# An attention, expert-mix and gated-product chain on one core: who straightens whole tiles, where positions are clipped, and the order of gathers and stores at the end of the expert stage

## The chip, the cores and the metric

The kernel runs on one core of one Trainium2 chip. A NeuronCore has five engines with queues of their own: PE (TensorE, matrix products into PSUM), DVE (VectorE), ACT (ScalarE), POOL (GpSimd) and SP (SyncE, which here only issues transfers). Each engine works through its own list in order; an instruction that has to wait holds up all that stands behind it on its engine. The metric is the device time of one execution in microseconds (us), lower being better.

## The reference, cut to what matters

Everything is float32. Linear attention (8 batches, 8 heads, 576 rows, 64 columns) makes x with 4608 rows and 512 columns. A router sends every row to two of eight experts, and a gated product follows:

```python
noisy_logits = x @ w_gate + log1p(exp(x @ w_noise)) * noise
top2, top2_w = two largest of noisy_logits, softmax over the two
for e in range(8):                      # w1[e]: 512x1024, w2[e]: 1024x512
    out[mask] += top2_w[mask, k, None] * (np.maximum(x[mask] @ w1[e], 0.0) @ w2[e])
a = x @ w1; b = x @ w2                  # the second stage: moe2_w1, moe2_w2
return ((a * b) @ w3) @ w_out
```

## The kernel before

**Stages.** The generator `front` does attention and routing. The experts run as *units*: a unit is two or three tiles of 128 routed rows of one expert (`cuts`, L662). Expert 0 is split into two halves: its first half list (rows of the first 18 row tiles) is units 0 and 1 and starts while attention still runs; its last half list is units `nu-2` (three tiles) and `nu-1` (two tiles), the last two of all. Experts 1 to 7 lie between, four units each. The gated product (`gated`) then runs over 12 blocks of three row tiles. Every product is three float32r matmuls (`mm3`, L97 to L100: high times high, high times low, low times high), so each operand is first split in two by `split` (ACT writes the high part, DVE the low part).

**Where rows come from.** Attention writes its rows to the DRAM tensor `X`; experts fetch rows by an indirect DMA on POOL's queue. Units 0 to 2 fetch a whole row tile in one indirect DMA (L709, `na` = 2, so `u <= na`); later units fetch four quarters of 128 columns (`gather_quarters`, L137), laid out so that one DVE transpose per tile suffices (L117). A whole tile is instead *straightened* first: POOL copies it with its columns regrouped into a tile `xr` (L122), PE transposes it in four pieces into PSUM (L124), and `split` makes `xT` of it. `xr` takes its buffers from the pool of the expert outputs (`y`, two buffers).

**The expert stage.** `unit` does `product1` eight times (steps 0 to 7, PSUM tiles `ph`, of which four can be in flight from unit 2 on), then `product2` per tile (steps 8, 9, 10, PSUM tiles `py`), whose result ACT copies to a tile `y` (L749) and stores to the DRAM tensor `Y` from ACT's own queue (L751). Between steps, `turn` straightens or transposes tiles of the next unit, `wstep` splits the next weights, and `hook_conv` does pieces of a conversion of the second stage's weights on DVE (L628 to L645).

**What leads over to the gated product.** `columns` (L877) runs once, behind unit `na+3`: it clips the rows' places in `Y` (`pos`, L879), spreads them over the partitions with 32 small matmuls (`replicate`, L132) and makes the gather indices `posq`. `gather2(i)` (L945) fetches the two expert results of each row of row tile i out of `Y`: eight indirect DMAs on POOL. `take(i)` weighs and adds them (ACT L957, DVE L960), transposes and splits them, and then issues `gather2(i + 2)`. The program calls `gather2(0)` and `gather2(1)` inside `w34` (a product of the second stage's weights, before unit `nu-2`), `take(0)` at step 9 of unit `nu-2`, `take(1)` at step 2 and `take(2)` at step 7 of unit `nu-1`, and the takes of block b+1 behind steps 1, 5 and 8 of block b (`CFB`).

**What orders the work.** The framework puts a wait between two accesses of the same tile or DRAM tensor, in the order in which the program writes them. A gather reads `Y` as a whole, so it waits for the stores written ahead of it, and a store waits for the gathers written ahead of it. Up to the end of unit 1 a scheduler merges the engines' lists; from L872 on the order is the program's own.

Of the kernel before, what the change touches and what calls it, by code (L numbers as in the profile page):

```python
# [8 lines left out]
F32 = mybir.dt.float32  # L9
# [6 lines left out]
ALU = mybir.AluOpType  # L16
# [8 lines left out]
D = NH * DH  # L25
E = 8
F = 1024
CU = 10
ROWS = 128 * CU
# [7 lines left out]
RTAIL = 4  # L37
PUMP = 3
CFB = {1: 0, 5: 1, 8: 2}
GROUPS = [(0, 9), (9, 15), (15, 18), (18, 26), (26, 32), (32, 35), (35, 36)]  # L40


@with_exitstack
def moe_chain_kernel(ctx, tc, q, kt, v0, v1, noise, wg, w1, w2, mw1, mw2, mw3t, mwo, out):
    nc = tc.nc
    V, A, P, G = nc.vector, nc.scalar, nc.tensor, nc.gpsimd
# [14 lines left out]
    pos = const.tile([128, NT, 2], F32, name="pos")  # L61
# [15 lines left out]
    rawp = pool(main, "rawp", 2)  # L77
# [32 lines left out]
    def by_chunk(rows):  # L110

        return rows.rearrange("p (i c d) -> p c i d", i=4, c=4)

    def transp(src, xt, t, quarters):
        if quarters:
            pt = extra["xq"].tile([128, 4, 4, 32], F32, name="xq", tag="xq")
            V.transpose(out=pt, in_=src.rearrange("p (j c d) -> p c j d", j=4, c=4))  # L117
            pt = pt.rearrange("p c j t -> p c (j t)")
        else:
            pt = ptr.tile([128, 4, 128], F32, name="pt", tag="pt")  # L120
            rows = late["y"].tile([128, 4, 4, 32], F32, name="xr", tag="y")
            G.tensor_copy(out=rows, in_=by_chunk(src))  # L122
            for c in range(4):
                P.transpose(pt[:, c, :], rows[:, c].rearrange("p i d -> p (i d)"), ident)  # L124
        split(pt, xt[:, 0, :, 128 * t:128 * t + 128], xt[:, 1, :, 128 * t:128 * t + 128])
# [16 lines left out]
    def front(st):  # L142
# [287 lines left out]
        def route(gi):  # L430
            i0, i1 = GROUPS[gi]
            n = i1 - i0
# [124 lines left out]
        for i in range(NT + 1):  # L557
# [7 lines left out]
            if i:  # L565
                q_logit(i - 1)
                if gi < len(GROUPS) and i == GROUPS[gi][1]:
                    rq.append(route(gi))
# [89 lines left out]
    def wtile(p):  # L658
        return p.tile([128, 2, 1024], F32R, name="w", tag="w")
# [11 lines left out]
    na = 2 * NS  # L671
    extra = {}
    raws, xg, xts = {}, {}, {}
# [44 lines left out]
    def xpose(u, t):  # L718
        if t == 0:
            xts[u] = late["xt"].tile([128, 2, 4, 384], F32R, name="xT", tag="xT")  # L720
        transp(xg.pop((u, t)), xts[u], t, u > na)

    def turn(u, step):
        n, e, part, j0, nt, N, first, last = units[u]
# [28 lines left out]
    events = {}  # L753
# [122 lines left out]

    def columns():  # L877

        V.tensor_scalar(out=pos, in0=pos, scalar1=float(E * ROWS - 1), scalar2=None, op0=ALU.min)  # L879
        V.tensor_scalar(out=posq, in0=replicate(pos.rearrange("p n k -> p (n k)")), scalar1=4.0,  # L880
                        scalar2=quart[:, 0:1], op0=ALU.mult, op1=ALU.add)
        V.tensor_copy(out=gwq, in_=replicate(gw.rearrange("p n k -> p (n k)")))
# [16 lines left out]
    def wscratch(key, k, p):  # L899
        w = wtile(p)  # L900
        nc.sync.dma_start(out=w.rearrange("p s f -> p (s f)").bitcast(F32), in_=WS[k])
        wt[key] = w
# [39 lines left out]
    BT = 3  # L942
    x2s = {}

    def gather2(i):  # L945
        if i >= NT:
            return
        for k in range(2):
            y = extra["g2"].tile([128, D], F32, name="yg", tag="yg")
            gather_quarters(y, Y, posq[:, :, 2 * i + k:2 * i + k + 1])  # L950
            x2s[i, k] = y

    def take(i):
        y0, y1 = x2s.pop((i, 0)), x2s.pop((i, 1))
        for j in range(4):
            c = slice(128 * j, 128 * j + 128)
            A.mul(out=y0[:, c], in_=y0[:, c], mul=gwq[:, j, 2 * i:2 * i + 1])  # L957
        for j in range(4):
            c = slice(128 * j, 128 * j + 128)
            V.scalar_tensor_tensor(out=y0[:, c], in0=y1[:, c], scalar=gwq[:, j, 2 * i + 1:2 * i + 2],  # L960
                                   in1=y0[:, c], op0=ALU.mult, op1=ALU.add)
        b, t = divmod(i, BT)
        if t == 0:
            xts["g", b] = late["xt"].tile([128, 2, 4, 384], F32R, name="xT", tag="xT")
        transp(y0, xts["g", b], t, True)
        gather2(i + 2)

    def load_b():
        for j in range(4):
# [1 line left out]

    nu = len(units)
    events[nu - 3, 7] = [w34_begin]
    events[nu - 2, 9] = [lambda: take(0)]
    events[nu - 1, 2] = [lambda: take(1)]
    events[nu - 1, 7] = [lambda: take(2), load_b]
    for u in range(na, nu):
        if units[u][2] == 2 and units[u][7]:
            unit_open(u, hook_conv)
        else:  # L980
            unit(u, hook_conv, True)
        if u == na:
            turns["py"].append(ptr)
        if u == na + 3:
            columns()
        if u == nu - 3:
            w34()
    for j in range(4):
        wscratch(("w", j), 20 + j, late["w2"])

    most = nc.values_load(nmax[0:1, 0:1], min_val=0, max_val=T)

    def gated():
        N = 128 * BT
        nblk = NT // BT
        ap_ = extra["a"]
        for b in range(nblk):
            xt = xts.pop(("g", b))
            pT = late["ht"].tile([128, 2, 8, 384], F32R, name="hT", tag="hT")
            for fb in range(8):  # L1000
                f0 = 128 * (fb % 2)
                for g in ("a", "b"):
                    ps = bank_of("ph", [128, 384])
                    w = wt[g, fb // 2].rearrange("p s (c f) -> p s c f", c=4)
                    for c in range(4):
                        mm3(ps, w[:, 0, c, f0:f0 + 128], w[:, 1, c, f0:f0 + 128], xt[:, 0, c, :], xt[:, 1, c, :],
                            c == 0, c == 3)
                    if g == "a":
                        a = ap_.tile([128, 384], F32, name="a", tag="a")
                        A.copy(out=a, in_=ps)  # L1010
                    else:
                        V.tensor_tensor(out=a, in0=a, in1=ps, op=ALU.mult)  # L1012
                        split(a, pT[:, 0, fb, :], pT[:, 1, fb, :])
                if b + 1 < nblk and fb in CFB:
                    take(BT * (b + 1) + CFB[fb])
            for m in range(BT):
                po = bank_of("py", [128, 512])
                for fb in range(8):
                    w = wt["w", fb // 2].rearrange("p s (c d) -> p s c d", c=2)
                    mm3(po, pT[:, 0, fb, 128 * m:128 * m + 128], pT[:, 1, fb, 128 * m:128 * m + 128],  # L1020
                        w[:, 0, fb % 2, :], w[:, 1, fb % 2, :], fb == 0, fb == 7)
                y = late["y"].tile([128, D], F32, name="y", tag="y")
                A.copy(out=y, in_=po)
                r = N * b + 128 * m
                nc.sync.dma_start(out=out[r:r + 128, :], in_=y)
                if b + 1 < nblk and m + 8 in CFB:
                    take(BT * (b + 1) + CFB[m + 8])

    gated()
    main.close()  # L1030

# [124 lines left out]
```

## Time and profile before

| | us |
|---|---|
| median of three runs (1743.00 to 1746.36) | 1745.32 |
| the profiled execution | 1746.65 |
| its span, first to last instruction | 1744.7 |
| PE busy | 1665.7 (95%) |
| DVE, ACT, POOL busy | 886.3, 572.5, 690.7 |

The sum of the prediction is made against the profiled execution, whose span leaves 1.95 us around it. PE's granted clock is 0.982 of full speed over the whole span. All times of rows below are counted from the span's start. Unit 0 begins near 153 us, unit 2 near 262, unit 6 near 375, unit `nu-2` near 1066, unit `nu-1` near 1099 and the gated product near 1131. A timeline row ends in brackets with the idle time of the engine just before it and what ended it.

### The profile page before, as it was taken

The page shows a single profiled execution, that of the slowest core. Times are in us where ns is not written, and L with a number is a line of the kernel's source. Part 1 is how long each engine was busy: PE and PEld are TensorE (multiplying, and loading weights), DVE is VectorE, ACT ScalarE, POOL GpSimd, SP SyncE. Part 2 cuts the span into 40 slices and gives each one's busy share as a digit, 9 for nine tenths or more (in the row PEclk, how much of TensorE's full clock was granted, in tenths as well). Part 3 has the DMA queues.
Part 4 walks back from the last instruction along what each step waited for, and adds up shares of the span by engine and source line. Part 5 has one row for each costly group of instructions (what it writes and reads, how often), then busy time and mean ns, then how long its engine had stood idle before and what let it go on. Part 6 is the DMA issues. An engine that isn't in the chain of part 4 may idle for free. (4 is left out here: it accounts for less than half of the span.)

```text
span 1744.7 us, 26430 instructions
## 1 busy us (share of the span) xinstructions
PE 1665.7 (95%) x9903; PEld 1519.5 (87%) x9903; DVE 886.3 (51%) x2251; ACT 572.5 (33%) x1195; POOL 690.7 (40%) x706
## 2 busy tenths in 40 slices
PE   6887979989999999999999999899999999999998
PEld 5666868988989989899998988789999999999997
DVE  6699735766567575774767513233323233332321
ACT  6553322333233333332333312232223233232321
POOL 4456334414334143341443420544454454444500
PEclk9898989999999999999999999999999999999999
DMA  8875344535355253553545484521111111111100
GB/s 297 263 238 173 110 151 150 175 104 168 112 169 172 86 177 124 162 157 104 166 152 173 154 318 165 187 101 43 49 53 48 52 54 35 44 48 52 50 23 20
DMA packets 130060, 221.51 MB, mean 127 GB/s; under 512 B 18560, under 2 KB 65792, under 8 KB 126848
## 3 DMA queue, kind: packets, MB, share of 16 engines
q1 hardware_dynamic: 95040, 152.07, 26.7%
q0 software_dynamic: 19072, 39.88, 8.4%
q10 hardware_dynamic: 15808, 27.71, 4.3%
q8 instruction: 85, 1.39, 0.3%
q14 instruction: 55, 0.45, 0.1%
HBM read 152.22 MB, written 67.37 MB: 126 GB/s over the span
## 5 line engine op out<-in xcount | busy, mean ns | idle before, releaser
L98 PE MATMUL ph<-xT,w 128*128 128x384 f32 (+1 forms) x1792 | 576.2, 322 | 13.6 <-DVE hT L739 9.4
L99 PE MATMUL ph<-xT,w 128*128 128x384 f32 (+1 forms) x1792 | 574.6, 321 | 0.8 <-DVE xT L95 0.7
L100 PE MATMUL ph<-xT,w 128*128 128x384 f32 (+1 forms) x1792 | 574.0, 320 | 0.0
L137 POOL DMA_INDIRECT xg<-X,idxq x288 | 282.5, 981 | 467.7 <-DVE xq L117 395.3
L137 POOL DMA_INDIRECT yg<-Y,posq x288 | 295.0, 1024 | 364.9 <-DVE yg L960 209.0
L98 PEld LDWEIGHTS ph<-xT,w 128*128 128x128 f32 x1792 | 339.8, 190 | 18.6 <-DVE hT L739 11.8
L100 PE MATMUL py<-w,hT 128*128 128x512 f32 x904 | 353.0, 390 | 0.4
L99 PE MATMUL py<-w,hT 128*128 128x512 f32 x904 | 352.3, 390 | 0.0
L98 PE MATMUL py<-w,hT 128*128 128x512 f32 x904 | 352.2, 390 | 0.0
L99 PEld LDWEIGHTS ph<-xT,w 128*128 128x128 f32 x1792 | 339.4, 189 | 3.3 <-DVE xT L95 1.5
L100 PEld LDWEIGHTS ph<-xT,w 128*128 128x128 f32 x1792 | 339.5, 189 | 0.0
L100 PEld LDWEIGHTS py<-w,hT 128*128 128x128 f32 x904 | 169.7, 188 | 37.4 <-DVE hT L739 2.0
L99 PEld LDWEIGHTS py<-w,hT 128*128 128x128 f32 x904 | 169.7, 188 | 34.0
L98 PEld LDWEIGHTS py<-w,hT 128*128 128x128 f32 x904 | 169.7, 188 | 33.9
L1012 DVE TENSOR_TENSOR a<-a,ph 128x384 f32<-128x384 f32 x96 | 53.0, 552 | 281.6 <-PE ph L100 263.5
L739 DVE SCALAR_TENSOR_TENSOR hT<-ph,hT 128x256 fp32r<-128x256 f32 (+1 forms) x256 | 120.5, 474 | 103.4 <-ACT hT L738 100.4
L738 ACT ACTIVATE hT<-ph 128x256 fp32r<-128x256 f32 (+1 forms) x256 | 107.2, 426 | 158.1 <-PE ph L100 143.6
L95 DVE TENSOR_TENSOR xT<-xq,xT 128x512 fp32r<-128x512 f32 x108 | 74.8, 693 | 154.9 <-ACT xT L94 154.9
L749 ACT COPY y<-py 128x512 f32<-128x512 f32 x77 | 45.2, 587 | 258.0 <-PE py L100 214.4
L94 ACT CAST xT<-xq 128x512 fp32r<-128x512 f32 x108 | 67.0, 620 | 138.7 <-DVE xq L117 129.2
L94 ACT CAST hT<-a 128x384 fp32r<-128x384 f32 x96 | 49.4, 514 | 182.3 <-DVE a L1012 182.3
L95 DVE TENSOR_TENSOR w<-raw,w 128x1024 fp32r<-128x1024 f32 x72 | 88.8, 1236 | 11.7 <-ACT w L94 11.6
(203 smaller groups left out, 1529.5 us busy)
## 6 DMA issues: line engine op xcount, KB each, us to landing
raw<-in_w_dram SPq DMA_DIRECT2D x72, 512.0 KB, 4.1
w<-WS SPq DMA_DIRECT2D x24, 1024.0 KB, 6.6
WS<-hl SPq DMA_DIRECT2D x80, 256.0 KB, 2.8
Y<-y ACTq DMA_DIRECT2D x77, 256.0 KB, 2.5
k<-in_kt_dram SPq DMA_DIRECT2D x32, 288.0 KB, 4.4
q<-in_q_dram SPq DMA_DIRECT2D x36, 256.0 KB, 4.0
X<-xt SPq DMA_DIRECT2D x36, 256.0 KB, 2.4
out_dram<-y SPq DMA_DIRECT2D x36, 256.0 KB, 2.1
```

Source lines behind the costliest of these rows:

```text
L94: A.copy(out=hi, in_=src)
L95: V.tensor_tensor(out=lo, in0=src, in1=hi.bitcast(F32), op=ALU.subtract)
L98: P.matmul(ps, st_h, mv_h, start=first, stop=False)
L99: P.matmul(ps, st_h, mv_l, start=False, stop=False)
L100: P.matmul(ps, st_l, mv_h, start=False, stop=last)
L137: G.indirect_dma_start(out=dst[:, 128 * j:128 * j + 128], out_offset=None, in_=src[:].rearrange("t (i c) -> (t i) c", i=4), in_offset=bass ...
L738: A.activation(out=hT[:, 0, fb, :N], in_=ph[:, :N], func=AF.Relu)
L739: V.scalar_tensor_tensor(out=hT[:, 1, fb, :N], in0=ph[:, :N], scalar=0.0, in1=hT[:, 0, fb, :N].bitcast(F32), op0=ALU.max, op1=ALU.subtract)
L749: A.copy(out=by_chunk(y), in_=py.rearrange("p (c i d) -> p c i d", c=4, i=4))
L1012: V.tensor_tensor(out=a, in0=a, in1=ps, op=ALU.mult)
```

## The change

It has three parts. First, `transp` takes the straightening copy as an argument: units 0 and 1 get `A.copy` (ACT), unit 2 gets `V.tensor_copy` (DVE), later units keep the DVE transpose; POOL copies nothing. Second, the clip of `pos` moves out of `columns` to just behind unit `na`, three units ahead. Third, `gather2(2)` is issued at step 4 of unit `nu-2`, ahead of that unit's three stores, into a freed buffer of the raw weight pool (`rawp`); `gather2(3)` and `gather2(4)` follow behind the last unit's stores; takes 0 to 2 issue no gather any more; and the takes of block 0 of the gated product stand behind steps 4, 7 and 9 rather than 1, 5 and 8.

```diff
+CF0 = {4: 0, 7: 1, 9: 2}
 ...
-            G.tensor_copy(out=rows, in_=by_chunk(src))
+            straight(out=rows, in_=by_chunk(src))
 ...
-        transp(xg.pop((u, t)), xts[u], t, u > na)
+        transp(xg.pop((u, t)), xts[u], t, None if u > na else V.tensor_copy if u == na else A.copy)
 ...
     def columns():
-        V.tensor_scalar(out=pos, in0=pos, scalar1=float(E * ROWS - 1), scalar2=None, op0=ALU.min)
 ...
     def gather2(i):
+        if i == 2:
+            raw = rawp.tile([128, 2, D], F32, name="raw", tag="raw")
         for k in range(2):
-            y = extra["g2"].tile([128, D], F32, name="yg", tag="yg")
+            y = raw[:, k] if i == 2 else extra["g2"].tile([128, D], F32, name="yg", tag="yg")
 ...
     def take(i):
 ...
-        gather2(i + 2)
+        if i >= BT:
+            gather2(i + 2)
 ...
+    events[nu - 2, 4] = [lambda: gather2(2)]
     events[nu - 2, 9] = [lambda: take(0)]
 ...
         if u == na:
             turns["py"].append(ptr)
+            V.tensor_scalar(out=pos, in0=pos, scalar1=float(E * ROWS - 1), scalar2=None, op0=ALU.min)
 ...
+    gather2(3)
+    gather2(4)
 ...
+            turn_at = CFB if b else CF0
```

Unit 2's tiles on POOL, before: `xg` are fetched rows (L709 whole, L137 in quarters), `xr` the straightened copy. The second and third copies stand between the quarter gathers of later units.

```order
L709 DMA xg<-X,idx 128x512 x3
L122 COPY xr<-xg 128x512
L137 DMA xg<-X,idxq 128x128 x4
L122 COPY xr<-xg 128x512
L137 DMA xg<-X,idxq 128x128 x4
L122 COPY xr<-xg 128x512
L137 DMA xg<-X,idxq 128x128 x40
```

On DVE, the same place of the changed kernel (`hT`: split output of the first product, `xT`: split transposed rows). Before, the three `xT` rows stood together with no copy on this engine.

```order
L740 SCALAR_TENSOR_TENSOR hT<-ph,hT 128x256
L123 COPY xr<-xg 128x512 x2
L96 TENSOR_TENSOR xT<-pt,xT 128x4x128 x2
L123 COPY xr<-xg 128x512
L96 TENSOR_TENSOR xT<-pt,xT 128x4x128
L740 SCALAR_TENSOR_TENSOR hT<-ph,hT 128x384
L96 TENSOR_TENSOR w<-raw,w 128x1024
```

The copies have left POOL's list, where nothing but gathers is left, and the third one now stands behind the `xT` work of the first two tiles.

On ACT, units `nu-2` and `nu-1` before: the second tile's store and the three that follow it, with what each waits for. `DMASW` are POOL's gathers (eight counters, one per quarter), `DMAHW` the other transfers.

```order
L751 DMA Y_59<-y_12742 128x512 [waits DMAHW3_49,Activation_49]
...
L749 COPY y_12793<-py_12768 128x4x4x32 [waits DMAHW2_49,PE_49]
L751 DMA Y_59<-y_12793 128x512 [waits DMASW4_49,DMASW5_49,DMASW3_49,DMASW6_49,DMASW2_49,DMASW7_49,DMASW1_49,DMAHW5_49,DMASW0_49,Activation_49]
...
L749 COPY y_12994<-py_12969 128x4x4x32 [waits DMAHW3_49,PE_49]
L751 DMA Y_59<-y_12994 128x512 [waits DMASW4_49,DMASW3_49,DMASW5_49,DMASW2_49,DMASW6_49,DMASW1_49,DMASW7_49,DMASW0_49,Activation_49]
L749 COPY y_13022<-py_12997 128x4x4x32 [waits DMAHW5_49,PE_49]
L751 DMA Y_59<-y_13022 128x512 [waits DMAHW4_49,Activation_49]
```

The same five stores on ACT in the changed kernel, from the first of unit `nu-2` to the last of unit `nu-1`.

```order
L752 DMA Y_59<-y_12723 128x512 [waits DMASW4_49,DMASW3_49,DMASW5_49,DMASW2_49,DMASW6_49,DMASW1_49,DMASW7_49,DMASW0_49,Activation_49]
...
L752 DMA Y_59<-y_12751 128x512 [waits DMAHW3_49,Activation_49]
...
L752 DMA Y_59<-y_12792 128x512 [waits Activation_49]
...
L752 DMA Y_59<-y_12973 128x512 [waits DMAHW1_49,Activation_49]
...
L752 DMA Y_59<-y_13001 128x512 [waits Activation_49]
```

Only the first of them still waits for gathers, as it did before; the third and the fourth no longer do.

## Rows read from the trace of the kernel before

**Rows 1.** Waits of PE; columns: waiting line, releaser, total us, times, longest.
```profile
PE pt L124 <- POOL xr L122: 10.0, 3, 5.0
...
PE ph L98 <- DVE hT L739: 9.4, 2, 7.0
...
PE py L132 <- DVE pos L879: 4.7, 1, 4.7
...
PE ph L98 <- ACT a L1010: 2.9, 1, 2.9
```

**Rows 2.** Stretches: length; busy PE, PEld, DVE, ACT, POOL; clock; DMA share; GB/s.
```profile
0.00:153.00 153.00, 115.09 (x1180) 97.34 (x1180) 118.88 (x387) 88.86 (x184) 77.15 (x91) 0.92 0.80 260
...
248.20:261.80 13.60, 2.92 (x14) 1.87 (x13) 1.42 (x3) 2.34 (x4) 10.65 (x13) 0.66 0.19 58
261.80:266.20 4.40, 4.36 (x13) 3.96 (x14) 0.66 (x1) 0.00 (x0) 2.52 (x3) 0.50 0.22 60
...
372.80:374.90 2.10, 2.07 (x64) 1.91 (x64) 0.52 (x1) 0.00 (x0) 0.00 (x0) 0.50 0.83 243
374.90:378.90 4.00, 4.00 (x17) 4.00 (x14) 0.46 (x1) 0.00 (x0) 0.00 (x0) 0.51 0.03 8
379.00:1099.00 720.00, 719.39 (x4044) 650.37 (x4043) 428.30 (x998) 232.42 (x455) 247.99 (x253) 1.00 0.50 158
...
1112.10:1116.20 4.10, 4.05 (x19) 4.05 (x20) 3.38 (x10) 2.42 (x8) 1.82 (x2) 0.51 0.14 45
...
1143.40:1146.90 3.50, 3.50 (x14) 3.50 (x13) 2.89 (x8) 1.85 (x6) 0.21 (x1) 0.51 0.00 0
1147.00:1741.00 594.00, 591.46 (x3103) 556.87 (x3101) 184.01 (x382) 170.52 (x385) 255.93 (x248) 1.00 0.15 44
```

**Rows 3.** Timeline of PE before unit 2; columns: start, length, instruction, idle before.
```profile
248.76 0.66 PE L124 MATMUL pt<-ident,xr 128*128 128x128 f32 x4 [0.55 <-POOL xr L122]
...
261.79 0.69 PE L98 MATMUL ph<-xT,w 128*128 128x384 f32 x1 [0.68 <-ACT xT L94]
```

**Rows 4.** Timeline of POOL, the three copies of unit 2.
```profile
248.10 0.61 POOL L122 COPY xr<-xg 128x512 f32<-128x512 f32 x1 [12.63 <-DMA Y<-y]
...
253.70 0.62 POOL L122 COPY xr<-xg 128x512 f32<-128x512 f32 x1
...
259.32 0.61 POOL L122 COPY xr<-xg 128x512 f32<-128x512 f32 x1
```

**Rows 5.** Timeline of ACT in the same stretch.
```profile
248.87 0.33 ACTq L751 DMA_DIRECT2D Y<-y  x1
...
261.15 0.58 ACT L94 CAST xT<-pt 128x512 fp32r<-128x512 f32 x1 [5.03 <-PE pt L124]
```

**Rows 6.** Timeline of DVE in the same stretch.
```profile
250.08 0.69 DVE L95 TENSOR_TENSOR xT<-pt,xT 128x512 fp32r<-128x512 f32 x1 [9.36 <-ACT xT L94]
```

**Rows 7.** Stores of L751 between 225 and 262 us, time to landing.
```profile
DMA to landing us min/median/max: 2.0/2.1/4.5
```

**Rows 8.** Timeline of DVE: two small operations during POOL work.
```profile
135.09 3.25 DVE L269 TENSOR_SCALAR ks<-ks 128x4 f32<-128x4 f32 x1
...
231.43 0.19 DVE L859 CAST idxf<-idx 128x80 f32<-128x80 int32 x1
```

**Rows 9.** Timeline of POOL beside the second of these.
```profile
231.28 1.01 POOL L709 DMA_INDIRECT xg<-X,idx  x1 [2.29 <-DVE idx L501]
```

**Rows 10.** Timeline of ACT in units nu-2 and nu-1.
```profile
1111.26 0.94 ACT L738 ACTIVATE hT<-ph 128x256 fp32r<-128x256 f32 x3 [11.08 <-DMA yg<-Y,posq]
...
1140.22 0.58 ACT L749 COPY y<-py 128x512 f32<-128x512 f32 x1 [14.32 <-DMA yg<-Y,posq]
```

**Rows 11.** Timeline of POOL, first gather issued by take(0).
```profile
1098.07 0.94 POOL L137 DMA_INDIRECT yg<-Y,posq  x1 [47.45 <-DVE xq L117]
```

**Rows 12.** The chain of waits: start, length, the gathers' landing.
```profile
1106.81 3.90 DMA yg<-Y,posq
...
1133.78 5.91 DMA yg<-Y,posq
```

More of the change, by code (lines that the diff above doesn't have):

```diff
@@ L112, in by_chunk, with transp @@
         return rows.rearrange("p (i c d) -> p c i d", i=4, c=4)
-    def transp(src, xt, t, quarters):
-        if quarters:
+    def transp(src, xt, t, straight):
+        if straight is None:
             pt = extra["xq"].tile([128, 4, 4, 32], F32, name="xq", tag="xq")
@@ L964, in take @@
             xts["g", b] = late["xt"].tile([128, 2, 4, 384], F32R, name="xT", tag="xT")
-        transp(y0, xts["g", b], t, True)
-        gather2(i + 2)
+        transp(y0, xts["g", b], t, None)
+        if i >= BT:
+            gather2(i + 2)
     def load_b():
@@ L1013, in gated @@
                         split(a, pT[:, 0, fb, :], pT[:, 1, fb, :])
-                if b + 1 < nblk and fb in CFB:
-                    take(BT * (b + 1) + CFB[fb])
+                if b + 1 < nblk and fb in turn_at:
+                    take(BT * (b + 1) + turn_at[fb])
             for m in range(BT):
@@ L1025, in gated @@
                 nc.sync.dma_start(out=out[r:r + 128, :], in_=y)
-                if b + 1 < nblk and m + 8 in CFB:
-                    take(BT * (b + 1) + CFB[m + 8])
+                if b + 1 < nblk and m + 8 in turn_at:
+                    take(BT * (b + 1) + turn_at[m + 8])
     gated()
```

## The prediction, made before the changed kernel was run

> **What bounds the kernel now.** I read the table of stretches first, to see where PE falls short. In 379 to 1099 us PE is busy 719.39 of 720.00, and in 1147 to 1741 it is busy 591.46 of 594.00, at full clock [rows 2]. There only fewer matmuls would save time, and the change removes none. What can be saved lies in the gaps between, and the list of PE's waits names them: 10.0 us for the straightened copies of POOL, 4.7 us for the clip of `pos`, and two waits of 7.0 us (the longest of a group of 9.4) and 2.9 us that are put down to DVE and ACT [rows 1]. The rows of ACT say what these two are: ACT stood still for 11.08 and 14.32 us, both times until a gather out of `Y` had landed [rows 10]. Those are the stores of units `nu-2` and `nu-1`, which wait for gathers written ahead of them, with `hT` and `a` queued behind them on ACT. All three parts of the change aim at one of these gaps. After each gap PE runs for a while at half clock (0.50 or 0.51 in four stretches) [rows 2], so that a gap costs more than its length.
>
> **Part 1a, copies of units 0 and 1 on ACT.** Five copies of some 0.6 us leave POOL and go to ACT, which is busy 88.86 of the first 153 us, while DVE is busy 118.88 [rows 2] and nearly always in the last 70. The copies are not what PE waits for there. Two things can move the time. DVE loses time to POOL in places: an operation on four columns took 3.25 us [rows 8] while POOL worked through computing instructions, the first two copies at their end. And the scheduler lays DVE's and ACT's lists differently, so that such a collision can fall elsewhere, once more or once less. I count 0, with one such collision (about 3 us) either way, and 4 as the bad end, since `xT` of unit 0 now stands behind one more attention copy on ACT.
>
> **Part 1b, copies of unit 2 on DVE.** The first copy waits for a buffer of `y`, that is for a store to land, and started at 248.10; the second started at 253.70 and the third at 259.32 only because four gathers of 1.25 us each stood ahead of either on POOL ((253.70 - 248.10 - 0.61) / 4) [rows 4]. On DVE they no longer do. The new chain: copy 1 as before at 248.1. Copy 2 needs the other `y` buffer, whose store was issued at 248.87 [rows 5] and lands 2.1 us later (2.0 to 4.5) [rows 7], so it starts at 251.0. I take 0.55 us for a copy, a little under POOL's 0.61. PE's four pieces take 0.66 us at full clock [rows 3] and about twice that at half; ACT's high part takes 0.58 [rows 5], DVE's low part 0.69 [rows 6]. So: 251.0 + 0.55 + 0.9 + 0.6 + 0.7 = 253.8 for the low part of tile 2, behind which the third copy stands. Then 253.8 + 0.55 + 1.2 + 0.6 gives 256.2 for the first product of unit 2, against 261.79 [rows 3]: **5.6 us**. If PE's clock stays up over the shorter gap, 2.2 more come back (half of 4.40 us at 0.50 [rows 2]); PE is still idle for most of eight us, so I do not count that. If the store lands as late as 4.5 us, 2.4 are lost. Range 3 to 8. What follows unit 2's start (first `hT`, weight split, the conversion's first load) hangs on PE's first step and moves with it.
>
> **Part 2, the clip.** Between unit 5 and unit 6 PE waited 4.7 us for an operation on DVE [rows 1] that stood at the end of DVE's conversion work. Then the 64 small matmuls took 2.10 us at clock 0.50 and the first product step of unit 6 took 4.00 us at 0.51 [rows 2]. With `pos` clipped three units earlier PE goes straight on: 4.7 + 1.05 + 2.0 = 7.75 us. What is late next is DVE: it still finishes its conversion piece near 372.5 (the clip behind that ended PE's wait at 372.8) before it makes `posq` and `gwq` (about 1 us), so the first `hT` of unit 6 comes some 1.6 us later after PE's step than it did. Four `ph` tiles in flight, 2 us each, cover that with little to spare; I take off 0.25 and count **7.5 us**, range 5 to 7.75. The moved clip itself is one DVE operation of some 0.2 us in a unit where PE never waits: nothing.
>
> **Part 3, gathers and stores at the end.** Before, the first gather from `take(0)` started at 1098.07 [rows 11], and the third store of unit `nu-2` waited for the last of its eight to land: 3.90 us after the last began [rows 12]. The same again in `nu-1`, behind 16 gathers and a landing of 5.91 us [rows 12]. Now `gather2(2)` is written ahead of all three stores. Unit `nu-2` runs from 1066 to 1099, half of it in its eight steps of 2 us, half in three products of 5.5 us, so its first store is due near 1089. The buffer comes free with the unit's first weight split, behind step 0 or 1 (1070 to 1073); eight gathers take 10 us and land 3.9 to 5.9 later [rows 12], by 1084 to 1089. The next work behind that store on ACT is due only 5 us after it, so even 4 us of lateness cost nothing. The other four stores wait for no gather. Gone are 7.0 us of waiting and half of 4.10 us at clock 0.51 behind it, then 2.9 us and half of 3.50 us at 0.51: 7.0 + 2.0 + 2.9 + 1.7 = **13.6 us** [rows 1, 2].
>
> What is late next is block 0 of the gated product. A block takes about 50 us (594 us for somewhat under twelve [rows 2]); five of its eight double steps are 0.42 of its columns, so `take(3)` comes about 21 us, `take(4)` 33 and `take(5)` 44 us after PE's last expert matmul. Gather 3 can begin when the last store has landed: 0.6 us of copy, 0.4 of issue, 2.0 to 4.5 to land [rows 7], so at 3.0 to 5.5; it ends 10 us later and lands after 3.9 to 5.9 more [rows 12], at 17 to 21. Gather 4 follows by 27 to 31. Gather 5 is issued by `take(3)` behind gather 4, and lands at 39 to 43. All are in time by a hair or more, and ACT may be held for some 5 us before PE runs out of `ph` tiles. Price 0, range 0 to 4.
>
> **The sum.** 0 + 5.6 + 7.5 + 13.6 = 26.7 us off the profiled 1746.65: 1719.95. The median of the runs stands 1.33 lower, so I forecast **1719 us** for the median. With the good ends (3 + 8 + 7.75 + 13.6) it would be 1713; with the bad ends together (-4 + 3 + 5 + 9.6) 1732.
>
> **A rule that speaks against part 1b.** A DVE cast beside a running gather took 0.19 us [rows 8, 9], the usual time for its size, so gathers did not hold DVE up there. The Trainium skill says otherwise in its page SBUF — State Buffer, section "SBUF: two separate sides": DVE and GpSimd share one port pair as an exclusive lock, a float32 copy within SBUF takes it, and whoever comes first keeps it while the other blocks, descriptor writing included. That row disagrees for a small cast; for a copy of 512 columns no row here shows it.
>
> **The rivals.**
>
> *DVE's copies are held up behind POOL's gathers.* For it speaks that DVE did stand still for 3.25 us behind a run of POOL's instructions [rows 8]; against it the 0.19 us beside a gather. If copies 2 and 3 each wait for a run of four gathers, they start where POOL's did, and 5.6 becomes 0.5: 1745.32 - 21.6 = 1724.
>
> *The gathers behind the last store come late.* Eight loads of weights share the DMA engines with them, and the landing already rose from 3.90 to 5.91 us in that traffic [rows 12]. If gather 3 and those behind it come 10 us late, ACT holds PE for about 5 of them, and PE then loses about 2 more to the half clock: 1726.
>
> *Slower.* The same place, far worse: `take(3)` to `take(5)` stand in ACT's list ahead of everything that empties `ph`. Each us of lateness beyond about 5 costs one. To eat all 26.7 us the gathers would have to be some 32 us late (for instance if they waited for all weight loads and were then served one by one); at 37 us the time is 1750. The longest landing of these rows is 5.91 us, so this is remote.
>
> *The change doesn't do what it says.* If the stores still waited for gathers as long as before, and the copies too, only the clip would be left, 1738; with a front that lost 4 us it would be within 0.2% of before.
>
> **How the numbers follow.** Chances: forecast as reckoned 0.74, copies held 0.10, late gathers 0.09, no change 0.03, slower 0.04. The forecast's own range is 1713 to 1727 (not all bad ends at once), and both of the first rivals lie in it or at its edge; so 1712 to 1730 holds a little over 8 in 10, with the chance of several bad ends together outside. About 0.2%, 3.5 us, is what a measurement of this kernel can tell from no change. Faster by more 0.93, within it 0.03, slower 0.04.
>
> **What the new profile would show.** Part 1b: no PE wait for `xr` above 2.5 us and unit 2's first product about 5.6 us earlier against the end of unit 1. Part 2: no PE wait at the 64 small matmuls, and clock 1.0 there. Part 3: no ACT idle time put down to a gather in units `nu-2` and `nu-1`, and PE unbroken from 379 us on to the end. Part 1a: unit 0's start within 3 us of 153. The forecast is wrong if PE shows a new wait in block 0 behind `take(3)` to `take(5)`, if DVE's copies take more than 1 us each, or if the first stretch of attention grows.

## The result, and the profile after

The changed kernel took **1717.1 us** (median of 4 runs, 1714.79 to 1723.12); the kernel before took 1744.73 us (1743.00 to 1746.36) in the runs beside it. The ratio is 0.9847, with a 95% interval of 0.9818 to 0.9876. The profiled run of the changed kernel took 1719.07 us, its span 1717.3 us, against 1746.65 and 1744.7 us before: 27.4 us less of span.

The line numbers below are those of the changed kernel, mostly one higher than before. PE's waits first (waiting line, releaser, total us, times, longest); these are the rows that answer to [rows 1]:

```profile
PE pt L125 <- DVE xr L123: 3.0, 3, 1.8
PE ph L99 <- DVE hT L740: 2.6, 2, 2.4
...
PE ph L99 <- ACT xT L95: 1.2, 2, 0.7
```

The wait for the straightened copies fell from 10.0 us to 3.0. The waits for the clip (4.7), for `hT` behind the held ACT (7.0, the longest of the 9.4) and for `a` (2.9) are gone. What `hT` still shows, 2.4 us, is another place, near 270 us, where DVE waits for the conversion's first load.

The stretches of the changed kernel (length; busy PE, PEld, DVE, ACT, POOL; clock; DMA share; GB/s) answer to [rows 2]:

```profile
248.50:254.85 6.35, 2.64 (x14) 1.55 (x12) 2.59 (x6) 2.34 (x4) 3.99 (x5) 0.83 0.23 72
254.85:259.30 4.45, 4.41 (x13) 4.01 (x14) 0.67 (x1) 0.00 (x0) 3.54 (x4) 0.50 0.22 59
...
361.30:366.00 4.70, 4.70 (x86) 4.43 (x84) 4.46 (x15) 2.01 (x4) 0.00 (x0) 1.00 0.61 191
366.00:1085.00 719.00, 718.45 (x4037) 649.44 (x4037) 428.84 (x1000) 231.53 (x454) 254.93 (x260) 1.00 0.50 160
1085.00:1107.00 22.00, 22.00 (x146) 20.10 (x145) 8.10 (x20) 7.61 (x20) 0.00 (x0) 1.00 0.69 252
1107.00:1150.00 43.00, 43.00 (x234) 41.39 (x232) 13.72 (x28) 12.62 (x28) 25.41 (x26) 1.00 0.39 130
```

Of the places that the change aims at, PE still stands in one, before unit 2, and the 4.45 us at clock 0.50 behind it are as long as they were before (4.40 in [rows 2]). At unit 6, in unit `nu-1` and in the first gated block PE is busy without a break, at full clock, where the kernel before had its three other stretches at 0.50 and 0.51.

The starts of PE's products in the two traces give the length of each part of the program. I worked this table out from them (us; 390 products are about 73 us of gated work). The two columns on the right are traces of the same two kernels on another chip, the fourth, to which the experiments come:

| from ... to | before | changed | before, chip 4 | changed, chip 4 |
|---|---|---|---|---|
| start ... first product of unit 0 | 153.4 | 154.7 | 159.4 | 154.6 |
| ... last product of unit 1 | 94.5 | 93.6 | 94.6 | 93.7 |
| ... first product of unit 2 (part 1b) | 14.0 | 6.5 | 13.1 | 5.2 |
| ... last product of unit 5 | 105.9 | 106.3 | 106.0 | 107.8 |
| ... 13th product of unit 6 (part 2) | 11.2 | 3.6 | 10.6 | 3.6 |
| ... first product of unit `nu-2` | 687.5 | 687.5 | 706.2 | 706.8 |
| ... first product of unit `nu-1` | 33.0 | 33.0 | 33.0 | 33.0 |
| ... first gated product (part 3) | 31.2 | 22.1 | 29.3 | 22.1 |
| ... 390 gated products further (part 3) | 76.8 | 72.6 | 80.6 | 86.5 |
| ... last product | 530.7 | 530.7 | 530.7 | 530.7 |

On the first chip the differences are +0.5 for the first two rows together, -7.5 for the gap before unit 2, +0.4 for what follows it, -7.5 for the clip, and -9.1 and -4.2 (13.3) for the gathers. They add up to the 27.4 us. All other stretches are equal to a few hundredths.

### The profile page after: what moved, and what is told of

Same layout as the page of the kernel before. It is cut to its first block, busy times and chain, and to the rows that moved or that the text cites. A ratio compares the mean times of both kernels' runs of the same rounds, so it can differ in the third digit from the quotient of the medians.

```text
span 1717.3 us, 26430 instructions
## 1 busy us (share of the span) xinstructions
PE 1662.4 (97%) x9903; PEld 1516.9 (88%) x9903; DVE 881.7 (51%) x2254; ACT 575.6 (34%) x1200; POOL 682.1 (40%) x698
## 5 line engine op out<-in xcount | busy, mean ns | idle before, releaser
L138 POOL DMA_INDIRECT yg<-Y,posq x280 | 285.2, 1019 | 330.4 <-DVE yg L962 174.0
L740 DVE SCALAR_TENSOR_TENSOR hT<-ph,hT 128x256 fp32r<-128x256 f32 (+1 forms) x256 | 120.7, 474 | 89.2 <-ACT hT L739 86.5
```

Of the source, the lines that this page charges most:

```text
L138: G.indirect_dma_start(out=dst[:, 128 * j:128 * j + 128], out_offset=None, in_=src[:].rearrange("t (i c) -> (t i) c", i=4), in_offset=bass ...
L740: V.scalar_tensor_tensor(out=hT[:, 1, fb, :N], in0=ph[:, :N], scalar=0.0, in1=hT[:, 0, fb, :N].bitcast(F32), op0=ALU.max, op1=ALU.subtract)
```

## The experiments

The experiments ran on three chips, called second, third and fourth here. The kernel before took 1773.32, 1769.94 and 1769.72 us on them, 25 to 29 us more than beside the first result. The chip of that first result is not on record; that it was yet another one is inferred from these times. So totals are compared on one chip alone, and the three places by the length of the stretch.

### One part undone (second chip)

In the first, unit 2's copies go back to POOL:

```
-        transp(..., None if u > na else V.tensor_copy if u == na else A.copy)
+        transp(..., None if u > na else G.tensor_copy if u == na else A.copy)
```

> The changed kernel with unit 2's three straightening copies back on POOL; all else as changed. By the two traces the first product of unit 2 came 13.96 us after the end of unit 1 before and 6.50 us after it now, so I expect 7.5 us back: some 20 us faster than before, where the changed kernel is 27 us faster. My prediction had counted 5.6 us for this part (then 22 us faster than before). A rival, that the copies on DVE are held up by POOL's gathers and win nothing, would leave 27.

It took 1757.07 us, 0.9908 (0.9886 to 0.9931) of the kernel before. Its waits of PE between 230 and 300 us:

```profile
PE pt L125 <- POOL xr L123: 9.6, 2, 4.8
```

The old wait is back, and the gap before unit 2 is 13.0 us, against 5.1, 5.5 and 5.7 in the three other kernels of this chip. So this part is worth 7.4 to 7.9 us, as expected. The total is not: the kernel was 16 us under the kernel before, where 20 were expected.

In the second, the clip goes back to where `posq` is made:

```
     def columns():
+        V.tensor_scalar(out=pos, in0=pos, scalar1=float(E * ROWS - 1), ..., op0=ALU.min)
...
-            V.tensor_scalar(out=pos, in0=pos, scalar1=float(E * ROWS - 1), ..., op0=ALU.min)
```

> The changed kernel with the clip of the places back inside the function that spreads them, behind unit 5. By the traces 10.94 us lay between the last product of unit 5 and the second product step of unit 6 before, 3.64 us now. I expect 7.3 us back, 20 us faster than before, with the 64 small matmuls and the first product step at half clock again. Rival: DVE's lag hides the clip anyway, then 27.

It took 1759.24 us, 0.9921 (0.9903 to 0.9940). PE's waits between 340 and 380 us:

```profile
PE py L133 <- DVE pos L880: 4.7, 1, 4.7
```

It is the row of [rows 1] again but for the line numbers. From the last product of unit 5 to the 13th of unit 6 it took 10.3 us, 3.6 in the others: 6.7 us. The 64 small matmuls had clock 0.50 again, but the product step behind them 0.67 and not 0.51, which is why it is 6.7 and not 7.3. Here, too, the total was 14 us under the kernel before and not 20.

In the third, gathers and takes stand in the old order:

```
-        if i == 2:
-            raw = rawp.tile([128, 2, D], F32, name="raw", tag="raw")
...
-        if i >= BT:
-            gather2(i + 2)
+        gather2(i + 2)
...
-    events[nu - 2, 4] = [lambda: gather2(2)]
...
-    gather2(3)
-    gather2(4)
...
-            turn_at = CFB if b else CF0
+            turn_at = CFB
```

> The changed kernel with the old order of gathers and takes at the end of the expert stage (gathers of tiles 2 to 4 issued by the takes, takes of block 0 at steps 1, 5 and 8). I expect 13.3 us back, 14 us faster than before, and PE's two waits of 7 and 3 us there again. Rival: the waits were only moved by the other parts and some of the 13.3 belongs to them; then less than 10 comes back.

It took 1752.41 us, 0.9871 (0.9846 to 0.9897), which is 21 us under the kernel before and not 14. The first wait of PE is back (window 1040 to 1260 us):

```profile
PE ph L99 <- DVE hT L740: 5.6, 1, 5.6
```

The kernel before shows 5.6 us for it too on the fourth chip, 7.0 on the first. The second wait, 3 us for `a`, is not listed; in its place stand 5.5 us of "issue", a wait for which the profile has no releaser. Unit `nu-1` is longer by 8.5 us (30.6 against 22.1), as it should be, but the next 390 products are *shorter* here than in the other three kernels of the chip: 81.2 us against 84.9 to 86.3. Of 13.3 us only 3.3 to 4.8 are left. This is a miss, and the last group of experiments is about it.

In the fourth, the copies of units 0 and 1 go back to POOL:

```
-        transp(..., None if u > na else V.tensor_copy if u == na else A.copy)
+        transp(..., None if u > na else V.tensor_copy if u == na else G.tensor_copy)
```

> The changed kernel with only the five copies of units 0 and 1 back on POOL. My theory is that these copies are not what PE waits for: the end of unit 1 came 0.5 us later with them on ACT, so I expect the time of the changed kernel within 2 us, 27 to 28 us faster than before. Rival: POOL's copies hold up DVE in the attention stage; then 3 us or more come back and it is 24 us faster or less.

It took 1750.48 us, 0.9884 (0.9848 to 0.9920). It is 23 us under the kernel before and not 27 to 28, which by the total alone would speak for the rival (24 or less). But the changed kernel did not run on this chip, so the total says little by itself. It stands 6.6 us below the first and 8.8 below the second of these kernels, about what those two had undone. Units 0 and 1 took 94.9 us, between the 93.7 and 95.6 of the others: no effect of this part shows.

### How much time the late takes leave (third chip)

The changed kernel itself, on that chip:

> The changed kernel once more, beside the ones below on the same chip. If the three gains (7.5 for the copies of unit 2, 7.3 for the clip, 13.3 for the tail) are what the change is worth, it lies some 27 to 28 us under the kernel before wherever it runs. If a part of the 27 came from the run and not from the edit, it lies under 22 us here.

It took 1753.82 us, 0.9915 (0.9899 to 0.9932): 16 us under the kernel before, so the condition in the last sentence of the expectation (under 22 us) is the one that came true. Beside it, the three takes of block 0 moved three, two and one steps forward:

```
-            turn_at = CFB if b else CF0
+            turn_at = CFB
```

> In block 0 ACT takes the gated rows at 8 matmul groups earlier in the order, as in block 1. In the changed kernel gather 3 of block 0 landed about 21 us after TensorE's last expert matmul of unit nu-1, and ACT's first take of it stands late enough that nothing waits. Theory (the late place of the takes is what makes the reordered gathers safe; TensorE has about 5 us of slack behind ACT there): ACT holds 13 to 14 us on that take, TensorE loses 8 to 10 us, so the kernel is 8 to 10 us slower than the changed one. Rival (the gathers are in time whatever the place of the takes): within 1 us of the changed kernel.

It took 1758.40 us, 0.9941 (0.9928 to 0.9954), 4.6 us more than the changed kernel, with intervals that overlap by a hair. The trace shows the loss where it was expected. ACT's rows of the take (start, length, instruction, idle before):

```profile
1136.47 0.40 ACT L959 ACTIVATE yg<-yg,gwq 128x128 f32<-128x128 f32 x1 [2.29 <-DMA yg<-Y,posq]
...
1146.38 0.62 ACT L95 CAST xT<-xq 128x512 fp32r<-128x512 f32 x1 [5.91 <-issue]
1146.91 0.47 ACT L1018 COPY a<-ph 128x384 f32<-128x384 f32 x1
```

and PE's longest wait between 1040 and 1260 us:

```profile
PE ph L99 <- ACT xT L95: 6.0, 1, 6.0
```

The take follows the landing of each quarter of the tile. ACT was free at 1134.18 and came to the copy that empties `ph` only at 1146.91. The cast alone came 12.2 us after ACT was free, and PE lost 6.0. So about 6 us are covered by the `ph` tiles in flight: the 5 us of the prediction's third part. The hold was a little under the 13 to 14 us expected, and the loss well under the 8 to 10. The rival theory, that the place of the takes doesn't matter, falls: the changed kernel has no such wait on this chip.

### What is left before unit 2 (third chip)

Here the straightened tiles take their buffers from another pool of two (`xq`) in place of `y`, and PE's transposes of them are written behind unit 1's first product instead of its last:

```
-            rows = late["y"].tile([128, 4, 4, 32], F32, name="xr", tag="y")
+            own = "xq" in extra
+            rows = (extra["xq"] if own else late["y"]).tile([128, 4, 4, 32], ..., tag="xq" if own else "y")
...
                 if m < nt - 1:
                     wstep(8 * n + 10 + 2 * m)
-                else:
-                    wstep(8 * n + 12)
                     for t in range(nu):
                         xpose(u + 1, t)
                         gather_next()
+                else:
+                    wstep(8 * n + 12)
```

> The straightened tiles of unit 2 get buffers of their own in place of two of the y buffers, and TensorE's transposes of them are put between the products of unit 1. In the changed kernel 6.5 us without matrix products remain between units 1 and 2, then 4.5 us at the lower clock. Theory (what remains is the first copy's wait for the store that empties the y buffer, and the second copy's wait for TensorE's transposes of the first, both of which move under the products of unit 1): the gap is under 1 us, the stretch at the lower clock is gone, and the kernel is 6 to 8 us faster than the changed one. Rival (TensorE's transposes take the same time wherever they stand, and the copies then hold VectorE's work of unit 1): 0 to 3 us faster.

It took 1749.73 us, 0.9890 (0.9872 to 0.9908), 4.1 us under the changed kernel, with intervals that overlap, where 6 to 8 were expected and a gap under 1 us. The transposes now stand among the products, but 4.0 us of gap are left, of which PE waited 3.6 for "issue". ACT's rows show what was late: the last cast of unit 2's rows, whose input PE had made by 244.5 us:

```profile
244.74 0.59 ACT L95 CAST xT<-pt 128x512 fp32r<-128x512 f32 x1 [1.75 <-PE pt L126]
251.80 0.59 ACT L95 CAST xT<-pt 128x512 fp32r<-128x512 f32 x1 [6.48 <-remote]
```

("remote" is a release that the profile can't put down to anything.) POOL was in a row of 12 gathers until 250.8 us, 1.0 us before that cast.

The next kernel has the same edit, and DVE's work on the conversion starts three steps behind its first two loads instead of right behind them:

```
         raws = [conv_load(cp, p) for p in pieces[:2]]
+        yield
+        yield
+        yield
```

> The same, and the conversion's first two loads are issued three steps before VectorE's first operation on them. In the changed kernel VectorE stood 4.9 us on that load at 262 to 267 us and TensorE 2.4 us behind it. Theory: 2 to 3 us faster than the one with the transposes between the products. Rival (TensorE's wait there comes from VectorE's other work in the same stretch): within 0.5 us of it.

It took 1753.28 us, 0.9909 (0.9893 to 0.9924): no faster than the changed kernel as a whole, and not the 2 to 3 us faster than the one above that were expected. Locally it did what was meant. The cast happened to come before ACT's long idle time (6.6 us, until 253.3), and PE's rows show no gap:

```profile
249.05 0.40 PE L101 MATMUL py<-w,hT 128*128 128x512 f32 x1
249.29 0.34 PE L99 MATMUL ph<-xT,w 128*128 128x384 f32 x1
249.46 0.34 PE L100 MATMUL ph<-xT,w 128*128 128x384 f32 x1
```

At 0.34 us each these products ran at full clock, where the first product of the changed kernel took 0.69. Gap plus unit 2 to 5 went from 111.9 us to 103.0; behind a slower unit 1 (95.2 against 93.7) 7.3 us are left. But from unit 6 to unit `nu-2` this trace needs 712.7 us against 707.6, so 5 of them are lost again. POOL has seven rows of 12 gathers between 268 and 949 us here, three in the changed kernel beside it; whether that is what costs the 5 us was not tested.

### Where the rest of the 27 us went (fourth chip)

> The kernel before, for its trace on the chip of the runs below. On two chips the kernel before took 1770 to 1773 us and the changed one 1754, 16 us less in place of 27; there TensorE's waits 'issue' (no releaser in the profile) came to some 20 us in the changed kernel, in stretches of up to 12 us at the end of bursts of 12 or more gathers, with products 0.7 or 1.4 us apart, and to 0.2 us in both traces of the first chip. Theory (the gathers put close together by the change set these stalls off): on such a chip the kernel before shows two stalls fewer between its last and the first gated products and some 10 us less of them in all; the stretch from the first product of unit 2 to the end of unit nu-3 is as long in both. Rival (the chip stalls both kernels alike and the three gains are smaller there): the same sum of stalls in both, and a local gain under 6 us in one of the three places. On a chip without such stalls: none in this trace, and 27 to 28 us between the two.

> The changed kernel, for comparison on the same chip: 16 us under the kernel before on a chip that stalls, 27 to 28 us under it on one that doesn't. The three local gains are the same on either: 6 to 9 us between units 1 and 2, 7.3 at unit 6, 8 to 9 between the first product of unit nu-1 and the first gated product.

The kernel before took 1770.53 us as one of these runs, the changed one 1753.52, 0.9918 (0.9903 to 0.9934) of it. The two right columns of the table above are their traces. Parts 1b and 2 are worth 7.9 and 7.0 us here, nearly as on the first chip. Part 3 is not. Unit `nu-1` by itself is 7.2 us shorter (8 to 9 were expected), but unit `nu-1` and the 390 products behind it took 109.9 us before and 108.6 in the changed kernel, a gain of 1.4 us where the first chip had 13.3. The two kernels need the same 706 to 707 us from unit 6 to `nu-2`, 19 us more than on the first chip.

The sum of the waits named "issue" does not tell the two kernels apart (14.3 us before, 13.8 in the changed kernel), so the rival is right on that count, and the theory's number for it was wrong. The stretch shows more than the waits, because products that come one at a time also cost clock. This is PE in the changed kernel on the fourth chip:

```profile
1149.90 0.34 PE L101 MATMUL ph<-xT,w 128*128 128x384 f32 x1
1150.07 0.34 PE L99 MATMUL ph<-xT,w 128*128 128x384 f32 x1
1150.99 0.33 PE L100 MATMUL ph<-xT,w 128*128 128x384 f32 x1 [0.58 <-issue]
1151.70 0.42 PE L101 MATMUL ph<-xT,w 128*128 128x384 f32 x1 [0.38 <-issue]
1151.96 0.34 PE L99 MATMUL ph<-xT,w 128*128 128x384 f32 x1
1153.10 0.33 PE L100 MATMUL ph<-xT,w 128*128 128x384 f32 x1 [0.80 <-issue]
1154.50 0.34 PE L101 MATMUL ph<-xT,w 128*128 128x384 f32 x1 [1.07 <-issue]
```

The products had started every 0.17 us; then they come up to 1.4 us apart. Its stretches at two such places, with the undisturbed one between them (columns as above):

```profile
1047.00:1054.00 7.00, 3.60 (x12) 2.04 (x11) 0.00 (x0) 0.34 (x1) 2.84 (x3) 0.93 0.15 37
1109.00:1149.50 40.50, 40.50 (x238) 38.60 (x237) 11.72 (x26) 10.82 (x26) 10.47 (x11) 1.00 0.63 235
1149.50:1159.00 9.50, 4.64 (x17) 3.17 (x16) 0.09 (x1) 0.48 (x1) 5.09 (x6) 0.81 0.17 44
```

In 9.5 us PE did 17 products, and DVE and ACT did next to nothing. The DMA engines were not full then: the only transfers of that stretch are the gathers', neither weights nor instructions were loaded (queue and kind: packets, MB, share of 16 engines):

```profile
q0 software_dynamic: 212, 0.41, 17.1%
```

What all such places have in common is POOL: in the traces of the three chips the long ones begin when POOL has issued 11 or more gathers without a pause and end 1 to 8 us behind the last. Here POOL's rows of 16 gathers lie at 1031 to 1051, 1136 to 1156 and 1162 to 1183 us. The third meets ACT: its copy of the second product of block 0's end, which PE had made by 1180.0 us, came 5 us late, `take(5)` stood behind it, and PE waited:

```profile
1185.23 0.59 ACT L1031 COPY y<-py 128x512 f32<-128x512 f32 x1 [10.03 <-remote]
```

```profile
1188.83 0.44 PE L99 MATMUL ph<-xT,w 128*128 128x384 f32 x1 [3.37 <-ACT xT L95]
```

Against the first chip the first 195 gated products lost 8.3 us (42.9 against 34.6) and the next 195 lost 5.7 (43.6 against 37.9).

To test whether the rows of gathers do this, 24 small copies on POOL are put behind the gathers of the gated tiles 0, 1, 3, 4 and 5, so that no more than 8 gathers follow each other there:

```
             x2s[i, k] = y
+        if i in (0, 1, 3, 4, 5):
+            for _ in range(24):
+                G.tensor_copy(out=extra["pz"], in_=ident)
```

> The changed kernel with 24 small copies on GpSimd (some 4 to 5 us) behind each of the gated tiles 0, 1, 3, 4 and 5, so that no burst there is longer than 8 gathers. Theory (bursts of 12 and more gathers set the stalls off): on a chip that stalls, the stretches at 1046, 1149 and 1185 us are gone or under 2 us each, and the kernel is 12 to 18 us faster than the changed one; the stalls in the units before, whose bursts are not split, stay. Rival (the stalls hang on the place in the program or on the chip alone): they stay, and the kernel is within 2 us of the changed one or up to 5 us slower, since gather 5 lands some 5 us after ACT wants it. On a chip that doesn't stall: 0 to 5 us slower.

It took 1766.18 us, 0.9987 (0.9974 to 0.9999): 12.7 us *slower* than the changed kernel. The expected gain of 12 to 18 us did not come; the reason can be read. Its stretches:

```profile
1047.00:1054.00 7.00, 7.00 (x32) 5.64 (x31) 1.34 (x2) 1.17 (x2) 5.47 (x6) 1.00 0.41 121
1109.00:1149.50 40.50, 40.50 (x219) 38.78 (x218) 12.53 (x25) 10.54 (x25) 16.81 (x34) 1.00 0.44 161
1149.50:1159.00 9.50, 9.50 (x48) 8.41 (x47) 2.73 (x6) 2.58 (x7) 7.43 (x11) 1.00 0.22 57
1168.00:1183.00 15.00, 3.90 (x13) 2.96 (x12) 2.82 (x6) 2.71 (x6) 11.92 (x24) 0.64 0.17 53
1198.00:1221.00 23.00, 7.72 (x23) 5.26 (x23) 2.57 (x5) 1.99 (x4) 13.71 (x15) 0.61 0.17 44
```

Both standstills that were shown are gone: PE is busy through 1047 to 1054 and 1109 to 1159 us, and the first 195 gated products took 34.6 us, as on the first chip, against 42.9 in the changed kernel beside it. But the pause was twice as long as meant:

```profile
1138.14 9.29 POOL L957 COPY pz<-ident 128x128 f32<-128x128 f32 x24
```

So ACT, free at 1164.5 us, came to the cast of tile 5 only at 1179.7, some 13 us late instead of 5, and PE waited for it at the end of block 0,

```profile
PE ph L99 <- ACT xT L95: 11.0, 1, 11.0
```

and POOL, behind by then, issued the next 24 gathers without a pause from 1186 to 1216 us. From 1199 to 1220 us PE has its longest standstill of all. Splitting the rows of gathers took two standstills away, and joining them brought another: the standstills follow the rows of gathers, not the place in the program. Why a row of gathers has this effect is not shown.

> The same pauses in the kernel whose transposes of unit 2 stand between the products of unit 1 and whose conversion loads are issued earlier. Theory: on top of the pauses, 8 to 9 us less between the last product of unit 1 and the end of unit 5 (5 of the gap, 4 of the wait for the conversion and of the lower clock), so 8 to 9 us under the one with the pauses alone, unless stalls of the units move. Rival (what is won there is lost again behind): within 2 us of it.

This one took 1769.15 us, 0.9994 (0.9978 to 1.0009), 3 us more than the one with the pauses alone. In its front there was a row of 12 gathers, ACT's last cast of unit 2 came at 259.86 us behind it, and PE lost 4.5 us before unit 2. Gap and units 2 to 5 together were 5.3 us shorter than in the run with the pauses alone (107.3 against 112.6), but units 0 and 1 were 5.2 us longer (98.8 against 93.6). So the same edit gave 7.3 us on the third chip and nothing here, where 8 to 9 were expected. No version measured beats the changed kernel beyond doubt.

## Why the prediction was right, step by step

**The mechanism and the sum.** 26.7 us were forecast and 27.4 of span came, from the three places named. The old waits disappeared, and each part but 1a, undone by itself, brought back its own wait. That the sum came within 0.7 us is luck in part: 1b was 1.9 us too low, 1a and the rest together 1.2 too high.

**Part 1a** was counted at 0 within -4 to 3. It shows 0.5 us of loss on the first chip and nothing on the second. Right, though the start of unit 0 alone varies from 152 to 159 us between the traces, so an effect of 2 us could not be seen.

**Part 1b** was counted at 5.6 and gave 7.5, inside its range. The step that failed is the second copy. The prediction had it wait for the store issued at 248.87 [rows 5] to land. These are DVE's copies in the changed kernel:

```profile
248.95 0.43 DVE L123 COPY xr<-xg 128x512 f32<-128x512 f32 x1 [7.49 <-DMA Y<-y]
250.12 0.43 DVE L123 COPY xr<-xg 128x512 f32<-128x512 f32 x1 [0.75 <-PE pt L125]
...
252.53 0.42 DVE L123 COPY xr<-xg 128x512 f32<-128x512 f32 x1
```

The first does wait for a store. The second waits for PE's transposes of the first, and starts 0.7 us after the last tile's store was issued at 249.39, before it could have landed (no store of [rows 7] took under 2.0): at 250.12 and not 251.0, though unit 1 ended 0.5 us later here than before. A copy took 0.43 us and not 0.55, and PE's second transposes were still at full clock (0.66 us, 0.9 reckoned). The chain behind the third copy was right: 2.3 us to the first product. The 2.2 us for the clock did not come back, as the prediction had it.

**Part 2** was counted at 7.5 and gave 7.5 (6.7 and 7.0 on other chips). PE's 64 small matmuls now take 0.71 and 0.68 us:

```profile
361.46 0.71 PE L133 MATMUL py<-pos,ident 128*32 128x72 f32 x32
361.99 0.68 PE L133 MATMUL py<-gw,ident 128*32 128x72 f32 x32
362.60 0.44 PE L99 MATMUL ph<-xT,w 128*128 128x384 f32 x1
```

DVE came to the first `hT` of unit 6 at 366.71, 4.1 us after PE's first product there, and PE has no wait: the tiles in flight covered it.

**Part 3** was counted at 13.6 and gave 13.3 on the first chip. ACT's idle time that ended with a gather, 11.08 and 14.32 us [rows 10], is gone. One size was off. The last store is this row of ACT,

```profile
1108.23 0.33 ACTq L752 DMA_DIRECT2D Y<-y  x1
...
1129.89 1.28 ACT L959 ACTIVATE yg<-yg,gwq 128x128 f32<-128x128 f32 x4
```

and the first gather behind it this row of POOL:

```profile
1116.90 0.94 POOL L138 DMA_INDIRECT yg<-Y,posq  x1 [49.00 <-DVE a L1020]
```

DVE had long been done, so what POOL waited for was the landing, which the trace puts 7.9 us after the store's issue where 2.0 to 4.5 was reckoned from [rows 7]. (On the fourth chip the same row names the store itself.) That is part of the way to the rival of the late gathers. It cost nothing because `take(3)` came at 1129.89, with no idle time ahead of it. The run with early takes showed the cover to be some 6 us, and the run with pauses what lies beyond it: PE lost 11.0 us. On the fourth chip the changed kernel itself shows the sign of being wrong that the prediction named, a new PE wait behind `take(5)` (3.4 us).

**The rivals.** In the changed kernel DVE's copies were not held up by POOL's gathers: the second and third took 0.43 and 0.42 us with a gather beside them, the first 0.43 with none. The rows of POOL beside the copies, from the same trace:

```profile
249.64 1.03 POOL L138 DMA_INDIRECT xg<-X,idxq  x1 [13.64 <-DVE xr L123]
...
252.22 0.95 POOL L138 DMA_INDIRECT xg<-X,idxq  x1 [0.30 <-issue]
```

The first of these gathers took 1.03 us, where most take 0.94 to 0.95. In other kernels of the experiments it was the copy that grew. The run with units 0 and 1 on POOL has one of 0.60 us that started 0.59 us behind a gather:

```profile
249.60 0.60 DVE L123 COPY xr<-xg 128x512 f32<-128x512 f32 x1 [0.86 <-PE pt L125]
```

```profile
249.01 0.95 POOL L138 DMA_INDIRECT xg<-X,idxq  x1 [12.63 <-DVE xr L123]
```

Six copies in these traces started 0.53 to 0.72 us behind a gather; they took 0.48 to 0.67 us, and every one ended 1.19 us behind the start of its gather. Copies that started at other moments of a gather took 0.42 to 0.44. So the two do keep each other waiting, but by at most 0.24 us a copy. Such an exclusion of a float32 copy and descriptor writing is what the Trainium skill describes (page SBUF — State Buffer, section "SBUF: two separate sides"); the traces agree with the exclusion, but not for the length of a whole gather, inside which the third copy above ran undisturbed. The small cast of [rows 8], which the prediction took as speaking against it, started 0.15 us into its gather, where no copy was held either. The rival needed a wait for four gathers, some 5 us, and falls.

**What the prediction could not see.** On the two other chips where the changed kernel ran it is worth about 16 us, not 27, and nothing in the trace of before, taken on the first chip, pointed to it (0.2 us of "issue" waits in either trace there). The forecast's own range, 1713 to 1727 us, stands for 18 to 32 us gained, so 16 would have missed it. The changed kernel gathers more densely behind unit `nu-1` than before, and on the fourth chip PE, ACT and DVE lose behind these rows of gathers nearly as much as part 3 had gained. That the rows set the standstills off is shown for two places by the run with pauses; what links the two is not.

## What to carry to other kernels

A wait that ends when a group of gathers has landed is removed by writing the gathers earlier, but on the chips of the experiments the time gained was not kept where they crowd: look at how long the row of gathers becomes, and at the slack of whoever takes them (6 us here), not at the wait alone. A change should be measured on more than one chip when its parts are worth less than one per cent, and then by the length of stretches between the same products. For a copy into a shared pool, look up which buffer each instance gets: the releaser may be one's own last user and not the store.

## What the runs showed of the hardware that was not expected

- In the traces of the three chips of the experiments, rows of 12 or more gathers on POOL came with a standstill of PE, ACT and DVE at their end that the profile puts down to "issue" or "remote": products up to 1.4 us apart instead of 0.17, 17 products in 9.5 us, an ACT cast held for 6.48 us. The DMA engines were 17% busy meanwhile, with gathers alone. With at most 8 gathers in a row two such standstills went. On the first chip 40 gathers in a row, from 1117 to 1168 us, did nothing of the kind. What differs between the chips, and what the engines lack meanwhile, stays open; the rows show only when.
- A store of 256 KB landed 7.9 us after its issue just behind seven weight loads of 1 MB each (issued 1091 to 1108 us), 2.0 to 4.5 in the stretch of [rows 7].
- A DVE copy of 128x512 that started 0.53 to 0.72 us into an indirect gather of POOL ended 1.19 us behind the gather's start: 0.48 to 0.67 us long, where it takes 0.43 alone.
- 24 copies of 128 columns took POOL 9.29 us, 0.39 each, while a copy of 512 columns took it 0.61 [rows 4]: a quarter of the columns cost nearly two thirds of the time.
